# Two of the four score tiles of each regular block in a row on TensorE, with new order keys for the regular blocks and for the first blocks

## The chip, the core and the metric

The kernel runs on one core of a Trainium2 chip. The metric is the device time of one execution in microseconds, the median of several runs. TensorE (PE in the rows) does the matrix products, VectorE (DVE) and ScalarE (ACT) read its results from PSUM, GpSimd (POOL) works in SBUF alone, and SyncE (SP) issues the DMAs.

## The reference

Single-head attention over 12,288 queries with keys and values that are pooled 4 x 4 from a 384 x 32 map and projected (768 of them), then two feed-forward layers of width 2048 with different activations:

```python
kv_flat = kv_pool.reshape(B, -1, C) @ w_sr      # 768 keys, C = 128
s = scale * (q @ kv_flat.T); a = exp(s - max); a /= a.sum + 1e-9
x = a @ kv_flat                                  # 12288 x 128
g = where(h >= 1, h, where(h <= -1, 0, (h + 1)**2 / 4))   with h = x @ w_in
x = g @ w_out
out = gelu_sigmoid(x @ w_in2) @ w_out2
```

## The kernel before

The queries are cut into 24 blocks of 512 rows. Every large product is made from a high and a low float32r part of each operand, so it takes three matmuls (`mm3`, lines 350 to 352 and, for the second product of a layer, lines 1244 to 1247). A block has this work on TensorE, in tasks that follow one another without a break inside:

- four score tiles of 128 queries by 768 keys (`scores`, tile S): six matmuls of 384 columns each;
- the product with the values (`pv`): three groups of six matmuls of 512 columns;
- for each of the two layers eight pairs of 128 hidden columns: the first product (`h_pair`, tile h, six matmuls of 512 columns) and the second (`o_pair`, tile acc, six matmuls of 512 columns, which add to one PSUM bank per layer). In the text h1 and h2 are the first products of layers 1 and 2, and an acc task is one `o_pair`.

PSUM has three places of two banks each (room "h") for S, h and pv together, and one bank for the acc of each layer. A score tile keeps its place until its maximum (DVE, line 743), its exponential (ACT, line 757), the division into a high part (ACT, line 1125) and the low part (DVE, line 1131) are done. An h1 keeps its place until the clip (DVE, line 1274), the square (ACT, line 1281) and the final minimum (DVE, line 1285) are done, an h2 until two activations (ACT, lines 1328 and 1334) are done. ACT needs another table for the exponential than for the activation of layer 2, and loads it at each change.

Blocks 0 to 3 are laid out differently (functions `first`, `early`, `once`), since the weights, which come as 64-bit floats, are converted to float32 at the same time (`unit`, DVE lines 587 to 606). Blocks 4 to 23 are the regular ones (`regular`).

The order of the instructions is made on the host ahead of the launch, by `Plan.order`. Every task has an engine, an estimated duration, the tasks that it comes after, the places that it takes, and a key. Whenever an engine is free in the plan, the ready task with the lowest key whose places are free goes next. The engines then run their own lists in this order. The key is a time on a raster of steps of 6.768 us (`STEP`), eight steps a block, plus an offset of the task's kind. For a regular block the offsets are `REG_AT` (where the block's scores begin, in steps), `ATT_KEY` (for score tiles: 0 is the distance of the second two tiles from the first two, 1 that of the two in a couple, 2 to 4 the offsets of maximum, exponential and reciprocal, 5 to 8 those of the division and the turning, 9 and 10 those of pv), `STEP_AT` (h2, acc of layer 1, acc of layer 2, in steps), `PAIR1` and `PAIR2` (the activations of the two layers) and `ENDS`. `FINE` adds a further offset to single tasks by number: most of those of the constants, weights and blocks 0 to 3, none of the attention of the regular blocks.

```python
base = ATT_AT[b] if b < len(ATT_AT) else at((b - 2) * NP + REG_AT)
_, r, sh = scores(b, t, base + ATT_KEY[0] * half + ATT_KEY[1] * u, ahead=ATT_KEY[2:5])
```

Of the kernel before, what the change touches and what calls it, by code (L numbers as in the profile page):

```python
# [23 lines left out]
    REG_AT=2.93,  # L24
    STEP_AT=(0.54, 2.45, 0.5),
    ATT_KEY=(26.49, 2.85, 18.08, 13.03, -19.64, 10.84, 4.1, -15.3, 8.86, 57.26, -2.82),
    PAIR1=(3.65, -0.48, 3.27, 7.62, -6.74),
    PAIR2=(1.57, -6.31, 2.52, 13.5),
    ENDS=(7.48, -5.42),
# [1417 lines left out]
```

## Time and profile before

| | |
|---|---|
| median of 3 runs | 1304.73 us (1303.97 to 1305.10) |
| profiled execution, its own time | 1305.31 us |
| its span, first to last instruction | 1303.6 us |
| TensorE busy | 1291.9 us, 99% |
| ScalarE busy | 1079.1 us, 83% |
| GpSimd busy | 939.9 us, 72% |
| VectorE busy | 910.2 us, 70% |
| mean granted TensorE clock | 0.995 |

The profile is of one execution. Matmul durations overlap, since the next starts while the last one drains, so the distance between starts is what a matmul costs. The profiled execution took 0.58 us longer than the median of the runs, and 1.7 us lie outside its span.

### The profile page before, as it was taken

Reading aid. Unit: us, or ns where it says so; the run is one execution under the profiler, and the core shown is the slowest. Engines: PE = TensorE matmul, PEld = TensorE weight load, DVE = VectorE, ACT = ScalarE, POOL = GpSimd, SP = SyncE. Lnnn points to the kernel's source line nnn. Section 1 sums busy time; section 2 is a strip of 40 time slices with the busy share of each in tenths; the row PEclk is TensorE's granted clock in tenths of the full one; section 3 lists DMA queues with packets and bytes.
Section 4 is the critical chain, followed back from the end, with each engine's and each line's share of the span. In section 5 each row is a group of like instructions: output and inputs, shape, how many; then the busy total and the mean of one; then the engine's idle time right before and its main releaser. Section 6 shows DMA issues by size and latency. Waiting matters only on the chain.

```text
span 1303.6 us, 16928 instructions
## 1 busy us (share of the span) xinstructions
PE 1291.9 (99%) x5907; PEld 1079.3 (83%) x5908; DVE 910.2 (70%) x1078; ACT 1079.1 (83%) x1265; POOL 939.9 (72%) x431
## 2 busy tenths in 40 slices
PE   9999999999999999999999999999999999999998
PEld 7868888888888888888888888888888888888886
DVE  4987676866777768767777677677776776775531
ACT  2878988888988888889888888898888888987765
POOL 4678886777766777777667767776677677766886
PEclk8999999999999999999999999999999999999999
DMA  9403155355445534554455344544553455333000
GB/s 339 147 9 93 22 172 135 105 150 148 124 114 168 133 111 114 150 146 117 113 170 136 108 120 146 144 115 113 170 138 105 128 146 144 100 106 105 1 9 17
DMA packets 166164, 157.42 MB, mean 121 GB/s; under 512 B 106304, under 2 KB 153024, under 8 KB 166080
## 3 DMA queue, kind: packets, MB, share of 16 engines
q1 hardware_dynamic: 165024, 156.21, 42.5%
q8 instruction: 48, 0.79, 0.3%
q14 instruction: 36, 0.29, 0.1%
q10 hardware_dynamic: 1056, 0.13, 0.1%
HBM read 85.52 MB, written 70.78 MB: 120 GB/s over the span
## 4 chain that ended last, share of the span: by engine, by line
PE 97%; DVE 1%; DMA 1%; issue 0%; SPq 0%; ACT 0%; DVEq 0%
PE h L350 13%; PE h L352 13%; PE h L351 13%; PE acc L1245 13%; PE acc L1247 13%; PE acc L1244 13%; PE S L350 3%; PE S L352 3%; PE S L351 3%; PE pv L352 2%; PE pv L351 2%; PE pv L350 2%; PE acc L1238 1%; PE pv L848 1%; DMA kv<-in_kv 1%
## 5 line engine op out<-in xcount | busy, mean ns | idle before, releaser
L346 POOL TENSOR_TENSOR glo<-u,ghi 128x1024 fp32r<-128x1024 f32 x350 | 837.0, 2409 | 300.4 <-ACT u L1334 135.1
L1274 DVE TENSOR_SCALAR u<-h 128x1024 f32<-128x1024 f32 x172 | 210.7, 1225 | 210.2 <-PE h L352 199.4
L1244 PE MATMUL acc<-ghi,O 128*128 128x512 f32 x752 | 293.7, 391 | 0.0
L1245 PE MATMUL acc<-ghi,O 128*128 128x512 f32 x752 | 293.3, 390 | 0.0
L1285 DVE SCALAR_TENSOR_TENSOR u<-h,u 128x1024 f32<-128x1024 f32 x192 | 233.7, 1218 | 82.1 <-ACT u L1281 76.1
L1328 ACT ACTIVATE ghi<-h 128x1024 fp32r<-128x1024 f32 x192 | 197.1, 1027 | 70.7 <-PE h L352 69.5
L1247 PE MATMUL acc<-glo,O 128*128 128x512 f32 x752 | 232.5, 390 | 0.0
L1281 ACT ACTIVATE u<-u 128x1024 f32<-128x1024 f32 x178 | 188.1, 1057 | 37.3 <-DVE u L1274 36.9
L1291 ACT ACTIVATE ghi<-u 128x1024 fp32r<-128x1024 f32 x184 | 194.8, 1060 | 7.2 <-PE acc L1245 3.5
L1334 ACT ACTIVATE u<-h 128x1024 f32<-128x1024 f32 x166 | 169.0, 1020 | 0.0
L1247 PEld LDWEIGHTS acc<-glo,O 128*128 128x128 f32 x752 | 141.1, 188 | 30.1
L1245 PEld LDWEIGHTS acc<-ghi,O 128*128 128x128 f32 x752 | 141.2, 188 | 27.3
L1244 PEld LDWEIGHTS acc<-ghi,O 128*128 128x128 f32 x752 | 141.2, 188 | 26.6
L350 PE MATMUL h<-xhi,W 128*128 128x512 f32 x384 | 151.2, 394 | 0.0
L351 PE MATMUL h<-xlo,W 128*128 128x512 f32 x384 | 149.7, 390 | 0.0
L352 PE MATMUL h<-xhi,W 128*128 128x512 f32 x384 | 149.7, 390 | 0.0
L351 PE MATMUL h<-x2lo,W 128*128 128x512 f32 x384 | 149.4, 389 | 0.0
L352 PE MATMUL h<-x2hi,W 128*128 128x512 f32 x384 | 149.4, 389 | 0.0
L350 PE MATMUL h<-x2hi,W 128*128 128x512 f32 x384 | 149.4, 389 | 0.0
L743 DVE TENSOR_REDUCE nm<-S 128x1 f32<-128x768 f32 x92 | 87.7, 953 | 9.3 <-PE S L352 7.0
L350 PEld LDWEIGHTS h<-xhi,W 128*128 128x128 f32 x384 | 72.1, 188 | 16.5 <-issue 1.3
L351 PEld LDWEIGHTS h<-xlo,W 128*128 128x128 f32 x384 | 72.1, 188 | 15.9 <-issue 0.7
(135 smaller groups left out, 1876.5 us busy)
## 6 DMA issues: line engine op xcount, KB each, us to landing
turned<-TT SPq DMA_DIRECT2D x82, 768.0 KB, 4.2
PT_lo<-turned SPq DMA_DIRECT2D x168, 192.0 KB, 4.6
PT_hi<-turned SPq DMA_DIRECT2D x160, 192.0 KB, 3.9
kv<-in_kv SPq DMA_DIRECT2D x12, 512.0 KB, 7.9
out<-o SPq DMA_DIRECT2D x94, 64.0 KB, 1.9
q<-in_q SPq DMA_DIRECT2D x92, 64.0 KB, 2.4
raw_W<-in_moe_w_in SPq DMA_DIRECT2D x8, 512.0 KB, 8.5
raw_O<-in_moe_w_out SPq DMA_DIRECT2D x8, 512.0 KB, 7.1
```

Source lines behind the costliest of these rows:

```text
L346: eng.tensor_tensor(out=lo, in0=full, in1=f32(hi), op=ALU.subtract)
L350: nc.tensor.matmul(ps, wl, xh, start=first, stop=False)
L351: nc.tensor.matmul(ps, wh, xl, start=False, stop=False)
L352: nc.tensor.matmul(ps, wh, xh, start=False, stop=last)
L1244: nc.tensor.matmul(acc, w[c][1], hi[:, c], start=k == 0 and c == 0, stop=False)
L1245: nc.tensor.matmul(acc, w[c][0], hi[:, c], start=False, stop=False)
L1247: nc.tensor.matmul(acc, w[c][0], lo[:, c], start=False, stop=k == NP - 1 and c == 1)
L1274: nc.vector.tensor_scalar(u, T["h", 1, b, k], -1.0, 1.0, ALU.max, ALU.add)
L1281: nc.scalar.activation(u, u, AF.Square, scale=1.0 if light else 0.5)
L1285: nc.vector.scalar_tensor_tensor(out=u, in0=T["h", 1, b, k], scalar=1.0, in1=u, op0=ALU.max, op1=ALU.min)
L1291: nc.scalar.activation(t, T["u", 1, b, k], AF.Copy)
L1328: nc.scalar.activation(t, T["h", 2, b, k], AF.Gelu_apprx_sigmoid)
```

## The change

Only the numbers in `ORDER` and `FINE` change: no task is added or taken away, and no duration, dependence or place. By the new keys the third and fourth score tiles of a regular block have the key steps 6.73 and 6.996 within their block and no h1 key (whole steps) between them; before they had 6.84 and 7.27, with the h1 key of step 7.0 between. The first and second tile have 2.99 and 3.25, before 2.93 and 3.35, with the h1 key of step 3.0 between them both times. The offsets of the other engines' tasks go from a few microseconds to hundreds, so that they work as ranks. Of `FINE` nearly all entries are new.

```diff
-    REG_AT=2.93,
-    STEP_AT=(0.54, 2.45, 0.5),
-    ATT_KEY=(26.49, 2.85, 18.08, 13.03, -19.64, 10.84, 4.1, -15.3, 8.86, 57.26, -2.82),
-    PAIR1=(3.65, -0.48, 3.27, 7.62, -6.74),
-    PAIR2=(1.57, -6.31, 2.52, 13.5),
-    ENDS=(7.48, -5.42),
+    REG_AT=2.99,
+    STEP_AT=(0.72, 1.72, 0.66),
+    ATT_KEY=(25.32, 1.79, -127.3, 116.38, -197.55, 82.12, -0.25, -285.85, -41.23, 2.7, -91.74),
+    PAIR1=(-299.59, 32.45, -80.73, -171.76, -17.68),
+    PAIR2=(28.1, -418.07, -297.44, 79.06),
+    ENDS=(368.8, -23.68),
...
-    0: -574.0, 1: 763.59, 4: 751.59, 5: -127.77, 7: -649.36, 8: -123.32, 10: -148.72, 12: 751.41, 13: -121.43,
+    0: -296.59, 1: 660.61, 4: 665.3, 5: -461.54, 7: -306.7, 8: -223.42, 10: -210.65, 12: 629.87, 13: -226.89,
...
```

## Rows read from the trace of the kernel before

**Rows 1.** Page: an engine's busy time; granted clock in 40 slices; the ending chain.
```profile
PE 1291.9 (99%) x5907; PEld 1079.3 (83%) x5908; DVE 910.2 (70%) x1078; ACT 1079.1 (83%) x1265; POOL 939.9 (72%) x431
PEclk8999999999999999999999999999999999999999
PE 97%; DVE 1%; DMA 1%; issue 0%; SPq 0%; ACT 0%; DVEq 0%
```
**Rows 2.** Busy time by stages: length, engines' busy us (instructions), granted clock, DMA share, GB/s.
```profile
14.00:30.00 16.00, 15.23 (x79) 14.34 (x79) 7.86 (x12) 5.40 (x15) 7.57 (x9) 0.68 0.93 337
30.00:62.00 32.00, 28.55 (x202) 25.84 (x203) 29.95 (x51) 27.52 (x58) 20.88 (x14) 1.00 0.57 183
46.00:54.00 8.00, 5.45 (x36) 4.28 (x35) 7.93 (x18) 7.11 (x15) 3.52 (x3) 1.00 0.22 38
62.00:130.00 68.00, 67.98 (x321) 52.79 (x320) 55.70 (x72) 55.48 (x76) 54.26 (x32) 1.00 0.17 48
616.00:668.00 52.00, 52.00 (x236) 43.65 (x235) 38.26 (x46) 44.75 (x52) 37.15 (x17) 1.00 0.47 132
1188.00:1240.00 52.00, 52.00 (x232) 43.03 (x231) 25.26 (x22) 36.54 (x39) 40.79 (x18) 1.00 0.03 6
```
**Rows 3.** Waits of TensorE, the three longest: us in total, times, longest.
```profile
PE A L984 <- DVE y L977: 1.4, 2, 0.9
PE S L350 <- ACT P L912: 1.4, 2, 0.9
PE T L836 <- ACT PTf L842: 1.2, 1, 1.2
```
**Rows 4.** TensorE in order of time near a single score tile: start us, us, instruction.
```profile
608.98 0.39 PE L1244 MATMUL acc<-ghi,O 128*128 128x512 f32 x1
...
611.02 0.39 PE L350 MATMUL h<-x2hi,W 128*128 128x512 f32 x1
...
611.70 0.33 PE L350 MATMUL S<-kT,qlo 128*128 128x384 f32 x1
...
612.77 0.39 PE L1244 MATMUL acc<-ghi,O 128*128 128x512 f32 x1
...
614.85 0.39 PE L350 MATMUL h<-xhi,W 128*128 128x512 f32 x1
```
**Rows 5.** TensorE in order of time, the one place with two score tiles in a row.
```profile
275.63 0.33 PE L350 MATMUL S<-kT,qlo 128*128 128x384 f32 x1
...
277.74 0.39 PE L350 MATMUL h<-xhi,W 128*128 128x512 f32 x1
...
279.13 0.39 PE L1244 MATMUL acc<-ghi,O 128*128 128x512 f32 x1
...
279.82 0.39 PE L1245 MATMUL acc<-ghi,O 128*128 128x512 f32 x1
...
284.58 0.39 PE L350 MATMUL h<-x2hi,W 128*128 128x512 f32 x1
```
**Rows 6.** DVE in order of time: the same two tiles' maxima and low parts.
```profile
276.90 2.00 DVE L743 TENSOR_REDUCE nm<-S 128x1 f32<-128x768 f32 x2 [2.34 <-PE S L352]
...
282.89 1.93 DVE L1131 SCALAR_TENSOR_TENSOR Pl<-S,rd,Ph 128x768 fp32r<-128x768 f32 x2
```
**Rows 7.** DVE and TensorE in order of time: the place of the tile of 611.70 comes free.
```profile
619.29 1.01 DVE L1131 SCALAR_TENSOR_TENSOR Pl<-S,rd,Ph 128x768 fp32r<-128x768 f32 x1
...
620.71 0.39 PE L350 MATMUL pv<-PT_hi,V 128*128 128x512 f32 x1
```
**Rows 8.** TensorE in order of time: two score matmuls of block 0 at the lower clock.
```profile
23.85 0.52 PE L352 MATMUL S<-kT,qhi 128*128 128x384 f32 x1
24.17 0.52 PE L350 MATMUL S<-kT,qlo 128*128 128x384 f32 x1
```
**Rows 9.** The end, in order of time: last turn on DVE, last stores.
```profile
1298.45 0.72 DVE L1380 STREAM_TRANSPOSE o<-acc 128x512 f32<-128x512 f32 x1 [10.36 <-PE acc L1247]
1299.19 0.85 SPq L1384 DMA_DIRECT2D out<-o  x2
```

193 rows, old and new, of the table FINE are left out of this document.

## The prediction

> **What bounds the kernel now.** I read the page's busy shares and its ending chain first. TensorE is busy 99% of the span and makes 97% of the chain that ended last [rows 1]; the reader is to see that nothing else is near. A mean hides stages, so the second view is the busy time by stage [rows 2]. From 62 us on TensorE has no gap: 67.98 of 68 us, then 52.00 of 52 in a regular stretch, and the same in the last blocks, where attention is over. Before that it has gaps: 28.55 busy of 32 us between 30 and 62, most of the 3.45 missing between 46 and 54 (5.45 of 8). There DVE is the full engine, 7.93 of 8 us. Between 14 and 30 the granted clock is 0.68, so part of that stage ran at 1.2 GHz, the rest at 2.4. The third view, TensorE's waits, has single waits of about 1 us, all of the start: for block 0's output on DVE, for the first exponentials, for the first evacuation [rows 3]. The end is one turn on DVE of 0.72 us and the last stores, 5.2 us after the last matmul [rows 9]; no key alters them.
>
> So the time is a start of some 62 us with at most a few microseconds of waits, and behind it a queue of matmuls whose number is fixed. The change only reorders. It can move the time in three ways: by what the order of matmuls itself costs, by new gaps in the full part, and by the start.
>
> **Score tiles in a row, the steady part.** The fourth view is TensorE in order of time. Nine undisturbed 512-column matmuls run from 608.98 to 611.02, that is 2.04 us or 227 ns each. A score tile runs from 611.70 to 612.77, 1.07 us for six matmuls of 384 columns. At the 227 ns for 512, 384 columns would be 170 ns and a tile 1.02, so each tile loses 0.05 us in itself. The nine matmuls behind it run from 612.77 to 614.85, 2.08 us, so another 0.04 us is lost after it [rows 4]. The kernel before holds one place where two tiles do stand in a row: twelve matmuls from 275.63 to 277.74, 2.11 us, and the nine behind them from 277.74 to 279.82, again 2.08 [rows 5]. Apart, two tiles cost 2 x (1.07 + 0.04) = 2.22 us; in a row they cost 2.11 + 0.04 = 2.15. One couple in a row thus saves 0.07 us (the rows are rounded to 0.01, so 0.05 to 0.09). There are 20 regular blocks, of which one has its couple already: 19 x 0.07 = 1.3 us, 1.0 to 1.7. This term lies wholly on the path, since TensorE is never idle there.
>
> The Trainium skill weighs against this term: "TensorE: Matmul & The Clock Gate", section Back-to-back issue gap, prices a matmul by its own columns alone, N / 2.4 + 2.5 ns; by that the neighbours don't matter and the change gives nothing in the steady part. The rows show 227 ns where its rule gives 216, and a cost that depends on what stood before, so I go by the rows; the rule's outcome is the rival (d).
>
> **The other engines' new ranks.** In a regular stretch of 52 us ACT is busy 44.75, DVE 38.26, POOL 37.15 [rows 2]: 7, 14 and 15 us are free in each block. Reordering their instructions costs nothing while this slack and the waiting acc tasks cover it. What they can cost is a PSUM place that comes free too late. The exponential's key goes from +13 to +116, so on ACT it stands behind almost every other ready task; the maximum, the reciprocal and the low part on DVE go to the front (-127, -198 and, by the sum of two offsets, about -204). These roughly balance within the tile's hold. The keys of acc of layer 1 move from 2.45 to 1.72 steps, so fewer acc tasks wait in reserve. The split of layer 1's result (`ENDS`, +7 to +369) becomes the last in rank on ACT; by the keys the first h2 that needs it stands two steps after the last acc of layer 1, some 13 us, which is its cover. SP's lists keep their keys but for the 1.17 us by which the second half comes earlier; pv's key falls from 57 to 3, but pv waits for its data anyway. DMA is at 0.47 in these stretches [rows 2]. I cost all of this at 0 as long as the cover holds; it is the work of rows 5 to 7 and I price its loss below.
>
> **The cover of a couple.** Where two tiles stood in a row, their places were taken from 275.63; the two low parts end the hold, two of them in 1.93 us from 282.89, so the first ends near 283.86 [rows 6]. TensorE meanwhile did the couple (2.11), one h1 (1.39) and four acc tasks, until 284.58 [rows 5]. It had 0.72 us of cover left and no gap. For a single tile the hold was 611.70 to 620.30 and the next user of a place started at 620.71 [rows 4, 7]: 0.41 us left. So the couple needs four acc tasks in reserve, as the plan had them there, and then is no tighter than the single tile.
>
> **The start.** Several hundred tasks, the conversions of the weights among them, have new `FINE` offsets. What the trace shows is the room: 3.45 us of TensorE idle between 30 and 62 against 2.05 us of DVE idle (29.95 of 32) [rows 2]. A better order on DVE could bring the work that TensorE waits for [rows 3] ahead of conversions that are needed later; at the best 3.45 us come back. A worse one has no such ceiling; the nearest price is the lower clock: a score matmul started every 0.32 us at 23.85 [rows 8] against 0.18 later [rows 5]. If eight more microseconds of work went at half speed, the start would lose 4 us. I take -0.4: nearer to zero than to either end, since DVE is at 94% of the stage and cannot be made to do more.
>
> **The sum.** Against the profiled execution: span 1303.6 - 1.3 - 0.4 = 1301.9; with the 1.7 us outside it 1303.6. That execution lay 0.58 us above the median, so the median to expect is 1303.0, 0.13% down. About 0.2%, 2.6 us, is what a measurement here can tell from no change: below 1302.1 counts as faster, above 1307.3 as slower.
>
> **Rivals.**
> (a) The start gives back more: the gaps of 46 to 54 close, 2.55 us [rows 2]. Then 1304.73 - 1.3 - 2.55 = 1300.9. For it: these waits are few and single [rows 3], and the whole early order is new. Against: DVE is at 7.93 of 8 there.
> (b) Slower: the couple outruns its cover. Two of three places are held at once, by tiles whose exponential now has the lowest rank. With three acc tasks in reserve instead of four TensorE would run dry at 284.58 - 1.36 = 283.22 and wait until 283.86 [rows 5, 6], 0.64 us; in each of 20 blocks that is 12.8 us, and 1304.73 - 1.3 + 12.8 = 1316.2. It decides from the point where the hold of the first tile exceeds 8.95 us with four acc tasks, or 7.59 us with three. Against: the couple of 275.63 had no gap [rows 5].
> (c) The start gets worse by a longer stretch at 1.2 GHz, 4 us: 1307.4. For: 14 to 30 stands at 0.68 already, with TensorE busy 15.23 of 16 us by its records [rows 2], so other pauses there may hold the lower level longer. The Trainium skill, same page, section Loop structure matters more than you think, lets the clock fall in a long wait between bursts. No gap of such length stands between 30 and 62 in this trace [rows 3].
> (d) No saving: tiles of a couple lose as much as two single ones, or something else goes between them because no place is free, as an acc task did behind the single tile [rows 4]. Then only the start is left: about 1304.3.
>
> **How the numbers follow.** The forecast (1303.0, itself 1302.0 to 1304.0) has a chance of 0.52, (a) 0.25, (b) 0.08, (c) 0.07, (d) 0.08. Faster by over 0.2%: (a) and a little of the forecast's lower edge, 0.29. Slower: (b) and (c), 0.15. Within: 0.56. The range takes in (a) with one more microsecond from the start, 1299.8, and reaches up to (c), 1307.4; left out are (b) and a very good start, some 0.14.
>
> **What would show it.** In the profile of the changed kernel: runs of twelve score matmuls of about 2.11 us, once a block, with about 2.08 us for the nine matmuls behind them; a period of a block shorter by 0.07 us; 52.00 of 52 busy still. (b) would show as waits of TensorE for DVE's low part or ACT, repeated some 20 times, and a stretch below 52.00; (a) and (c) in the first 62 us, by TensorE's idle time and the granted clock. The forecast is wrong if the point where TensorE becomes gapless moves by more than 2 us, or if the period changes by more than 0.1 us.

## The result and the profile after

| | before | after |
|---|---|---|
| median | 1304.86 us (4 runs) | 1321.29 us (1320.45 to 1323.04, 4 runs) |
| ratio | | 1.0129, interval 1.0111 to 1.0146 |
| profiled execution, its span | 1303.6 us | 1318.7 us |

The change makes the kernel slower by 16.4 us, above the range's upper end of 1307.4. The page of the kernel after, its line of engines and its chain that ended last, against [rows 1]:

```profile
PE 1298.5 (98%) x5907; PEld 1076.4 (82%) x5908; DVE 910.5 (69%) x1078; ACT 1078.4 (82%) x1265; POOL 938.7 (71%) x431
PE 90%; DVE 3%; ACT 3%; DMA 1%; SPq 1%; issue 0%; POOL 0%; DVEq 0%; ACTq 0%
```

The chain went through TensorE for 97% of the span; now it is 90%, and DVE and ACT have 3% each. The work is the same (x5907 matmuls). Where the time went is read from the stages (columns as in [rows 2]; the number behind an engine's busy time is how many instructions it had in the stage). The kernel after:

```profile
30.00:62.00 32.00, 29.14 (x201) 26.30 (x201) 29.87 (x52) 27.78 (x57) 21.28 (x15) 0.98 0.60 192
130.00:200.00 70.00, 69.79 (x315) 57.89 (x314) 45.55 (x52) 63.87 (x72) 56.26 (x24) 1.00 0.40 110
200.00:460.00 260.00, 260.00 (x1173) 218.36 (x1172) 190.52 (x224) 223.97 (x256) 187.50 (x82) 1.00 0.47 132
460.00:988.00 528.00, 521.86 (x2326) 431.72 (x2325) 382.19 (x449) 444.56 (x508) 368.14 (x160) 1.00 0.48 129
988.00:1032.00 44.00, 44.00 (x200) 37.01 (x199) 32.80 (x41) 38.06 (x44) 31.56 (x14) 1.00 0.38 106
1032.00:1188.00 156.00, 154.77 (x694) 128.71 (x694) 111.71 (x132) 129.88 (x149) 107.19 (x46) 1.00 0.46 126
1188.00:1240.00 52.00, 50.70 (x223) 41.33 (x222) 27.01 (x25) 37.91 (x41) 40.82 (x18) 1.00 0.23 61
```

The kernel before, the two late stages:

```profile
460.00:988.00 528.00, 528.00 (x2376) 443.21 (x2375) 390.46 (x462) 453.38 (x520) 377.10 (x163) 1.00 0.47 130
1032.00:1188.00 156.00, 156.00 (x702) 130.79 (x701) 114.64 (x134) 133.82 (x153) 110.06 (x48) 1.00 0.45 129
```

The reader is to see three things. The start is not to blame. From 200 to 460 us the changed kernel is as full as the old one, though its couples of score tiles are there. Then, from 460 us on, TensorE loses 50 matmuls of the 2376 that fitted before, 50 x 0.227 = 11.4 us, 8 more between 1032 and 1188, and 9 between 1188 and 1240 (223 against the 232 of [rows 2]): 67 x 0.227 = 15.2 us, the whole growth of the span. From 988 to 1032 nothing is lost. A steady kernel thus changes its pace in mid-run, three times. Busy time alone shows only 528.00 - 521.86 = 6.1 us of the 11.4, since a matmul's recorded 0.39 us reaches 0.16 us over the next one's start and covers short gaps; the count of instructions doesn't hide them.

The longest waits of TensorE after, in place of [rows 3]:

```profile
PE h L351 <- ACT u L1335: 5.0, 8, 0.7
PE h L351 <- DVE glo L347: 2.3, 7, 0.6
PE h L351 <- DVE u L1286: 1.5, 6, 0.3
```

All three are a first product h that waits for the last reader of an older h, so for a PSUM place. (L351 after is L350 before; the changed file is one line longer above it.) A good couple and the first bad one, TensorE in order of time, the kernel after:

```profile
430.89 0.39 PE L1245 MATMUL acc<-ghi,O 128*128 128x512 f32 x1
...
432.25 0.33 PE L351 MATMUL S<-kT,qlo 128*128 128x384 f32 x1
...
434.36 0.39 PE L351 MATMUL h<-xhi,W 128*128 128x512 f32 x1
...
441.20 0.39 PE L351 MATMUL h<-x2hi,W 128*128 128x512 f32 x1
...
482.85 0.39 PE L351 MATMUL h<-x2hi,W 128*128 128x512 f32 x1
...
484.21 0.33 PE L351 MATMUL S<-kT,qlo 128*128 128x384 f32 x1
...
486.32 0.39 PE L1245 MATMUL acc<-ghi,O 128*128 128x512 f32 x1
...
489.08 0.39 PE L351 MATMUL h<-xhi,W 128*128 128x512 f32 x1
...
500.79 0.50 PE L351 MATMUL h<-xhi,W 128*128 128x512 f32 x1 [0.67 <-ACT u L1335]
```

At 432 an acc task stands between the h2 and the couple; at 484 the couple follows the h2 at once. ACT in order of time tells what that does to the place of that h2 (its second activation gives it back):

```profile
432.02 1.02 ACT L1335 ACTIVATE u<-h 128x1024 f32<-128x1024 f32 x1
...
441.80 1.28 ACT L1329 ACT_TABLE_LOAD   x1
...
485.34 1.04 ACT L1292 ACTIVATE ghi<-u 128x1024 fp32r<-128x1024 f32 x1
486.28 1.01 ACT L1335 ACTIVATE u<-h 128x1024 f32<-128x1024 f32 x1
...
496.28 1.28 ACT L1329 ACT_TABLE_LOAD   x1
...
499.74 1.00 ACT L1335 ACTIVATE u<-h 128x1024 f32<-128x1024 f32 x1
```

In the good block the place is free 433.04 - 432.25 = 0.8 us after the couple's start, and the next h1 starts right behind the couple, at +2.1 us. In the bad block it is free at 487.29, 3.1 us after it; two of the three places are the couple's, TensorE does two acc tasks first, and the h1 starts at +4.9. Of the 2.3 us between 0.8 and 3.1, 1.36 us are the acc task that is missing ahead of the couple. The other 0.94 us are ACT's: it does a high part of layer 1 (485.34) between the two activations, which it does not at 432; without it the place would be free at about 485.34 + 1.01 = 486.35, just as the couple ends. Everything behind that h1 is later, its acc task too; ACT turns back to layer 2's table at 496.28, 12.1 us after the couple's start (at 441.80 in the good block, 9.6 us after it). The next matmul could have started at 499.96, but the h1 that TensorE's list has there waits until ACT is done with an h2, at 500.74.

**Why some blocks have the acc task there.** The key of h2 is `at(a) + 0.72 * STEP`, that of the acc task of layer 1 one step later `at(a - 1) + 1.72 * STEP`. On paper these are equal. In floating point they are not; the difference for the third pair of layer 2, whose keys stand just ahead of the couple's, worked out in double precision from the formulas of the code, is:

```
block of layer 2     key of h2 - key of acc   goes first   in the trace after
4, 5, 6              -5.7e-14                 h2           no gaps, 200 to 460 us
7 to 14              +1.1e-13                 acc          gaps, 460 us on
15, 16                0                       acc (added first)   gaps
17                   -2.3e-13                 h2           no gap, 988 to 1032 us
18, 19, 20            0                       acc (added first)   gaps
```

With h2 first, the acc task falls between it and the couple; with the acc task first, the couple follows the h2. The signs agree with the stages: TensorE has gaps where the acc task goes first, and none elsewhere. 13 blocks are bad, and the span grew by 15.1 us: 1.16 us for each.

The 13 are of two kinds, which take turns. In seven (couples at 484, 590, 697, 803, 909, 1068 and 1174 us) the couple stands in a row right behind the h2. In the six between them an acc task falls between the two tiles, and TensorE then waits twice for DVE:

```profile
537.45 0.33 PE L351 MATMUL S<-kT,qlo 128*128 128x384 f32 x1
...
538.52 0.39 PE L1245 MATMUL acc<-ghi,O 128*128 128x512 f32 x1
...
539.91 0.33 PE L351 MATMUL S<-kT,qlo 128*128 128x384 f32 x1
...
555.01 0.47 PE L351 MATMUL h<-x2hi,W 128*128 128x512 f32 x1 [0.26 <-DVE u L1286]
...
558.27 0.47 PE L351 MATMUL h<-xhi,W 128*128 128x512 f32 x1 [0.30 <-DVE glo L347]
...
590.51 0.33 PE L351 MATMUL S<-kT,qlo 128*128 128x384 f32 x1
```

The order that `Plan.order` gives for these keys, worked out from the code, has the acc task of the tie 9.6 us of plan time ahead of its h2 in those six, so there the last bit decides nothing. By the plan, then, they follow from the block before; no run separates the two. From 484.21 to 590.51 the two blocks take 106.30 us, where two full ones take 2 x 51.96 (from 380.29 to 432.25): one acc task on the wrong side of a couple costs 2.4 us over two blocks.

### The profile page after: what moved, and what is told of

Read it like the earlier page. It is cut to its first block, busy times and chain, and to the rows that moved or that the text cites. A ratio compares the mean times of both kernels' runs of the same rounds, so it can differ in the third digit from the quotient of the medians.

```text
span 1318.7 us, 16886 instructions
## 1 busy us (share of the span) xinstructions
PE 1298.5 (98%) x5907; PEld 1076.4 (82%) x5908; DVE 910.5 (69%) x1078; ACT 1078.4 (82%) x1265; POOL 938.7 (71%) x431
## 4 chain that ended last, share of the span: by engine, by line
PE 90%; DVE 3%; ACT 3%; DMA 1%; SPq 1%; issue 0%; POOL 0%; DVEq 0%; ACTq 0%
PE h L351 13%; PE h L353 12%; PE h L352 12%; PE acc L1245 12%; PE acc L1246 12%; PE acc L1248 12%; PE S L351 2%; PE S L353 2%; PE S L352 2%; PE pv L352 2%; PE pv L353 2%; PE pv L351 2%; DVE u L1275 1%; PE acc L1239 1%; PE pv L849 1%; DVE TT L1141 1%
## 5 line engine op out<-in xcount | busy, mean ns | idle before, releaser
L351 PE MATMUL h<-xhi,W 128*128 128x512 f32 x384 | 154.2, 401 | 6.5 <-ACT u L1335 4.8
L351 PE MATMUL h<-x2hi,W 128*128 128x512 f32 x384 | 150.2, 391 | 2.3 <-DVE u L1286 1.5
L353 PE MATMUL h<-xhi,W 128*128 128x512 f32 x384 | 149.9, 390 | 0.0
L351 PEld LDWEIGHTS h<-xhi,W 128*128 128x128 f32 x384 | 72.1, 188 | 28.8 <-ACT u L1335 7.9
L351 PEld LDWEIGHTS h<-x2hi,W 128*128 128x128 f32 x384 | 72.1, 188 | 20.3 <-PE h L353 3.9
```

The lines of the kernel that those rows point to most:

```text
L351: nc.tensor.matmul(ps, wl, xh, start=first, stop=False)
L353: nc.tensor.matmul(ps, wh, xh, start=False, stop=last)
```

## The experiments

All start from the changed kernel; the plan makes each order anew, so other tasks move a little too. Theory A below is the tie, B my rival (b) with the couple as such as its cause, C the new ranks.

**1. The tie settled for h2.**

```diff
-    STEP_AT=(0.72, 1.72, 0.66),
+    STEP_AT=(0.7199, 1.72, 0.66),
```

> The changed kernel with one key moved: the first product of layer 2 (h2) stands at 0.7199 steps instead of 0.72, so that it no longer ties with the acc task of layer 1 (1.72 steps, one step later), and goes first. Theory A (the tie, settled by the last bit of the key's sum, sends the acc task first in blocks from 460 us on and uses up the cover of the couple): no gap of TensorE behind 200 us, couples of score tiles in all regular blocks, and 1304.9 less 0.07 us for each of some 19 couples: 1303.5 us. Theory B (the couple as such outruns its cover, my rival b): gaps in every block with a couple, about 1.1 us in each, 1325 us or more. Theory C (it is the new ranks of ACT and DVE, the exponential behind all): unchanged, 1321 us.

Measured: 1305.12 us against 1304.34 before in the same job, ratio 1.0005 (0.9996 to 1.0014). All of the 16 us is back. The late stages are full, and the couple has its price of [rows 5]; stages and TensorE in order of time:

```profile
460.00:988.00 528.00, 528.00 (x2380) 443.59 (x2379) 391.87 (x462) 453.23 (x520) 377.20 (x163) 1.00 0.47 130
1032.00:1188.00 156.00, 156.00 (x703) 130.87 (x702) 115.19 (x135) 133.45 (x153) 110.12 (x48) 1.00 0.45 129
```
```profile
638.93 0.39 PE L1245 MATMUL acc<-ghi,O 128*128 128x512 f32 x1
...
640.29 0.33 PE L351 MATMUL S<-kT,qlo 128*128 128x384 f32 x1
...
642.40 0.39 PE L351 MATMUL h<-xhi,W 128*128 128x512 f32 x1
```

Couples in 18 blocks (12 in the changed kernel) and no gap behind 200 us: B as I had it falls, and so does C. The saving is there too. The first matmul of pv marks a block; eleven blocks apart, before and in this run:

```profile
464.63 0.39 PE L350 MATMUL pv<-PT_hi,V 128*128 128x512 f32 x1
1036.93 0.39 PE L350 MATMUL pv<-PT_hi,V 128*128 128x512 f32 x1
465.37 0.39 PE L351 MATMUL pv<-PT_hi,V 128*128 128x512 f32 x1
1036.93 0.39 PE L351 MATMUL pv<-PT_hi,V 128*128 128x512 f32 x1
```

A block takes 572.30 / 11 = 52.03 us before and 571.56 / 11 = 51.96 here: 0.07 us, as forecast. The median didn't reach 1303.5, though; the start keeps it (below).

**2. The tie settled for acc**, `STEP_AT=(0.7201, 1.72, 0.66)`.

> The changed kernel with the same key moved the other way, to 0.7201 steps: the acc task of layer 1 always goes ahead of h2. Theory A: the gaps that the changed kernel has from 460 us on (about 15 us in 13 blocks, 1.1 us a block) begin with the first regular blocks; five or six blocks more at 1.1 us give 1327 to 1329 us. Theory B and theory C: the tie is of no account, 1321 us.

Measured: 1327.80 us, ratio 1.0177 (1.0163 to 1.0191). The gaps now begin early and have the same three kinds:

```profile
200.00:460.00 260.00, 258.14 (x1157) 214.99 (x1156) 188.92 (x223) 220.91 (x253) 184.32 (x81) 1.00 0.48 131
```
```profile
PE h L351 <- ACT u L1335: 6.3, 10, 0.7
PE h L351 <- DVE glo L347: 2.8, 9, 0.6
PE h L351 <- DVE u L1286: 2.0, 8, 0.3
```

A ten-thousandth of a step, 0.7 ns on the raster, to either side decides over 22.7 us.

**3. One key in eight.**

```diff
-        hh, m = h_pair(2, b, k, t0)
+        hh, m = h_pair(2, b, k, t0 - (0.001 if k == 2 else 0.0))
```

> The changed kernel with the key of one h2 in eight moved by -0.001 us: that of the third pair, whose key stands just ahead of the couple of score tiles. Theory A in its narrow form (what matters is whether an acc task goes between that h2 and the couple): as with all eight moved, 1303.5 us and no gaps. Theory A in its wide form (each acc task that goes first uses up reserve): only part comes back, 1310 to 1318 us. Theory B and C: 1321 us.

Measured: 1305.89 us, ratio 1.0020 (1.0006 to 1.0034); its ten runs spread from 1304.50 to 1313.09. All stages behind 200 us are full, with the same count as in experiment 1:

```profile
460.00:988.00 528.00, 528.00 (x2380) 443.66 (x2379) 392.06 (x462) 453.05 (x520) 377.09 (x163) 1.00 0.47 130
```

The narrow form holds: what counts is the one tie ahead of the couple.

**4. The same keys, added up in another order.** No number changes:

```diff
-        t0 = at(a) + by_block("STEP_AT", b)[0] * STEP
+        t0 = at(a + by_block("STEP_AT", b)[0])
...
-        o_pair(1, b, k, at(a + LAG_O) + by_block("STEP_AT", b)[1] * STEP, [hi, lo], [ih, lh])
+        o_pair(1, b, k, at(a + LAG_O + by_block("STEP_AT", b)[1]), [hi, lo], [ih, lh])
```

> The changed kernel with every number as it is; only the sums that make the keys of h2 and of the acc task of layer 1 are taken in another order (the fraction is added to the step ahead of the multiplication), so that the two keys come out equal to the last bit wherever they are equal on paper, and the task that was added first, the acc task, goes first. Theory A: as with the acc task always first, 1327 to 1329 us, though no key has changed on paper. Any theory that rests on the values of the keys: 1321 us.

Measured: 1327.52 us, ratio 1.0176 (1.0159 to 1.0193), as with acc always first. The 1321 us of the changed kernel were a matter of rounding: a mixture of good and bad blocks.

**5. The place that this h2 holds.** From experiment 2, for the third pair of layer 2 the second activation reads the high part in SBUF instead of h, so the low part of this pair is no longer that of h:

```diff
+            src = f32(T["hi", 2, b, k]) if k == 2 else h
-            nc.scalar.activation(h if on_dve else T["u2", b, k], h, AF.Gelu_apprx_sigmoid)
+            nc.scalar.activation(h if on_dve else T["u2", b, k], src, AF.Gelu_apprx_sigmoid)
...
-        fu = add("ACT", act_us(2 * TB), t0 + PAIR2[1], full, after=[hi], uses=[hh], takes=[] if on_dve else [uh], table="gelu")
+        fu = add("ACT", act_us(2 * TB), t0 + PAIR2[1], full, after=[hi], uses=[ih if k == 2 else hh], takes=[] if on_dve else [uh], table="gelu")
```

> The second experiment's kernel (acc always first, 1327.8 us) in which the second activation of the third pair of layer 2 reads the high part in SBUF instead of h in PSUM, so that this h2 gives its place back one activation, about 1 us, earlier; its low part is then wrong. If what the gaps come from is the place that this h2 still holds when the couple starts, a good part of the 23 us comes back: 1310 to 1320 us. If it is the number of acc tasks in reserve alone, the place does not matter: 1326 to 1329 us.

Measured: 1317.24 us, ratio 1.0096 (1.0066 to 1.0125): 10.6 of experiment 2's 23 us come back, and of its waits the first is gone:

```profile
PE h L351 <- DVE glo L347: 2.3, 8, 0.3
PE h L351 <- DVE u L1286: 2.0, 8, 0.3
```

The wait that is gone is the one behind the couples, so there the held place is the cause. The two that are left stand in the blocks between (at 504.65 and 507.91 us, for one), where again no couple is in a row; why those stay, with the place given back early, wasn't separated.

**6. The couple taken apart**, from experiment 1: `ATT_KEY=(25.32, 2.85, ...` instead of 1.79.

> The first experiment's kernel (h2 key 0.7199, no tie) with the distance inside a couple of score tiles set back from 1.79 to 2.85 us, so that an h1 key lies between the third and fourth tile too. If the couple is the burden that the cover must carry (my rival b), taking the tiles apart can't hurt: 1304 to 1305 us, the couple's 1.3 us lost again. If the new ranks need the couple (both exponentials side by side, one change of ACT's table soon over), gaps come back without any couple: 1312 us or more.

Measured: 1317.81 us, ratio 1.0100 (1.0071 to 1.0129). No couple is left and the gaps are back, most of them too short to see as idle time: 526.95 busy of 528, but 2351 matmuls, 29 fewer than in experiment 1.

```profile
460.00:988.00 528.00, 526.95 (x2351) 436.96 (x2351) 382.82 (x452) 450.19 (x513) 372.16 (x162) 1.00 0.47 131
```

An example of a gap, in the same run:

```profile
554.81 0.61 PE L1248 MATMUL acc<-glo,O 128*128 128x512 f32 x2
555.50 0.50 PE L351 MATMUL h<-x2hi,W 128*128 128x512 f32 x1
```

Two acc matmuls of 0.227 us from 554.81 let the next start at 555.26; the h2 starts 0.24 us later, and only 0.08 us of that is idle time by the records. The couple is no burden here: with these ranks and these step offsets, tiles apart cost more than tiles together. It is not so for any step offsets: experiment 9 has the same ranks, its tiles apart, and no gap.

**7. The exponential's old rank**, from experiment 1: offset 13.03 instead of 116.38.

> The first experiment's kernel with the exponential's offset set back from 116.38 to 13.03 us, so that it goes ahead of most of ACT's ready work, as before the change. My step that the late rank of the exponential is a danger for the tile's place, balanced by DVE: with the earlier rank the places come free sooner, no gaps, 1304 to 1305 us. The other view: the exponential then changes ACT's table ahead of the activations of layer 2 that free the other places, and TensorE gets gaps, 1315 us or more.

Measured: 1334.52 us, ratio 1.0228 (1.0199 to 1.0258); TensorE's longest wait is now

```profile
PE h L351 <- DVE u L1286: 7.1, 19, 0.5
```

The late exponential, which I held for a danger, helps to keep the regular part full; bringing it forward costs 29 us. The couples go with it (one is left, at 282 us), and by experiment 6 that alone can cost 13 us with these keys; the two were not separated, nor was the table change shown to be the way.

**8. The old early offsets**, from experiment 1 with `FINE` of the kernel before.

> The first experiment's kernel with the old FINE offsets of the first blocks. If the early order is a matter of its own, worth within 1 us either way (the changed kernel's first 135 us lose as much to gaps as before, 15.2 us by distances of starts): 1304 to 1306 us. If the early offsets fit only the ranks with which they were set, the hand-over from block 3 to the regular blocks gets gaps between 100 and 400 us: 1310 us or more, with a gapless part behind it.

Measured: 1310.06 us, ratio 1.0040 (1.0020 to 1.0060). The loss stands at the hand-over, and the part behind is full:

```profile
200.00:460.00 260.00, 256.76 (x1147) 213.17 (x1147) 189.66 (x225) 218.24 (x250) 182.93 (x79) 1.00 0.50 140
460.00:988.00 528.00, 528.00 (x2381) 443.74 (x2380) 388.54 (x455) 454.86 (x521) 378.29 (x164) 1.00 0.47 132
```

The new early offsets are worth 5 us, as a fit to the new ranks and not as a better start.

**9. The old step offsets**, `STEP_AT=(0.54, 2.45, 0.5)`.

> The changed kernel with the old step offsets (0.54, 2.45, 0.5), all else new: the tie is gone, and so are nearly all couples of score tiles in a row, since the keys beside them have moved. Theory A: no gaps, and no saving of couples: 1304.8 us, about 1.2 us above the run with couples in all blocks, which measures the saving. Theory C (ranks of ACT and DVE): gaps as in the changed kernel, about 1321 us.

Measured: 1306.78 us, ratio 1.0011 (1.0003 to 1.0020), stages behind 200 us full, with one couple left:

```profile
460.00:988.00 528.00, 528.00 (x2378) 443.42 (x2377) 390.12 (x461) 456.20 (x521) 377.19 (x164) 1.00 0.46 130
```

That the ranks alone make gaps falls once more. The 1.7 us above experiment 1 can't be laid to the couples alone: the two differ at the start as well, so this run doesn't size the saving; the rows of experiment 1 do.

## Why the prediction was wrong, point by point

- **What bounds the kernel**: right. TensorE's list is the time, and the loss is gaps in it.
- **Score tiles in a row**, -1.3 us: the term held where the couple stands as I read it: 2.11 us for the twelve in experiment 1, and a block shorter by 0.07 us there, as I had it. The changed kernel has couples in 12 blocks only, experiment 1 in 18, not 20.
- **The start**, -0.4 us: wrong in sign, small. Between 130 and 200 us TensorE is busy 69.79 of 70 us, before 70.00. Experiment 1 has the couples' gain and no gap behind 200 us, yet its span is 1303.4 against 1303.6 before. Its 17 more couples are worth 1.2 us, so about 1 us went back ahead of 200 us, and its median is no better than before. At which point of the start it went was not isolated.
- **The other engines' ranks at no cost**: the step that failed, with the one that follows it. Put at 0 "as long as the cover holds", it measured some 15 us of late starts of TensorE behind 460 us (67 matmuls). I compared the step offsets one by one with the old ones and noted only that fewer acc tasks would wait in reserve. I worked out which keys lie between the couple's tiles, but not that 0.72 and 1.72 put h2 and acc on one and the same key just ahead of them. This stood in the diff.
- **The cover of a couple**: the sum of 8.95 us and the 0.72 us left were right for the couple at 275.63, and the one at 432.25 has 8.95 and 0.68 (its first low part ends at 440.52). The step was wrong in taking the surroundings of one couple of the kernel before [rows 5] as those of every couple after. Its "four acc tasks in reserve, as the plan had them there" depended on an acc task ahead of the couple, which the tie takes away. The place that ran short was not the couple's, either, whose hold I added up, but that of the h2 ahead of it and, 16 us on, those of later h1 and h2 tasks.
- **Rival (b)**: its kind was right, a place that comes free too late and TensorE without work, once a block; its sign, some 20 waits for DVE or ACT, came true with 8 + 7 + 6. That its 1316.2 us came near is luck, for its cause was not right: the couple as such has no gap (experiment 1), and with the same ranks and step offsets tiles apart have (experiment 6). Its price, 0.64 us in 20 blocks, was 1.16 us in 13. With a chance of 0.08 it was left out of the range.
- **Rivals (a) and (c)**: no stage at the start moved by their amounts. TensorE's busy time between 46 and 54 us rose by 0.87 us, not 2.55, and the clock between 14 and 30 was 0.72, not below 0.68.
- **Rival (d)**: no. Twelve together take 2.11 us, two single tiles 2.14 without what they cost the matmuls behind, and the block is shorter by 0.07 us. The formula of "TensorE: Matmul & The Clock Gate" of the Trainium skill, section Back-to-back issue gap, which I set behind it, is by that section's words the gap of an isolated matmul; for a stream, it says, weight load and matmul set the spacing together. So it was a weak ground for this rival, and the 227 ns of these rows are not its 216.

## What to carry to other kernels

When an order comes from keys, write the keys out on one axis and look for equal ones before looking at any duration: a tie is settled by rounding or by the order of creation, and can change from one loop turn to the next. Cover that was read off one place of a trace holds for another only if what stands ahead of it is the same. When the mean hides a change of pace, count an engine's instructions in equal stretches: 2376 against 2326 showed here what busy time showed by half. And where a plan carries its own estimates, look at where it ends: `Plan.order`, run on a host from the code, ends at 1301.8 us with the keys before, at 1331.2 with the changed ones, 1301.1 with 0.7199 and 1341.9 with 0.7201. These are the plan's estimates and no measurements, too large in the losses, but they tell the good keys from the bad; the prediction did not use them.

## What the runs showed that I had not expected

With TensorE full at 227 ns a matmul and three PSUM places, the order had almost no reserve: one acc task of 1.36 us on the wrong side of a couple cost 2.4 us over two blocks of 52 us, though ACT is busy only 86% and DVE 74% of a block. The block behind such a couple lost about as much as the block with it, without two tiles in a row of its own. And late starts that idle time nearly hides made up much of experiment 6's loss: 1.05 us of idle time between 460 and 988 us, but 29 matmuls or 6.6 us, of which the missing couples are some 0.7.
